# The last 64 rows of a Gram matrix on two 64-column tiles of the array, and its column sum on GpSimd

## Chip, cores, metric

One core of a Trainium2 chip; the three calls of experiments ran on two chips, each beside its own runs of the kernel before. The metric is device microseconds of one execution. All runs quoted here are in the fast state, with a granted TensorE clock of 0.999 or 1.0. Differences of a few tenths of a microsecond in 512 are at stake. The medians alone can't carry them, so the argument rests on stages of the trace: start times of single TensorE matmuls repeat within 0.02 us from run to run in all stages but the first.

## The reference, cut to what matters

```python
xn  = layernorm(x)                          # x: 2048 x 576
q, k, v = split(xn @ wqkv)                  # 32 heads of 18
phi = where(t > 0, t + 1, exp(t)) + 1e-6
kv  = phi(k)^T v     per head
z   = sum over tokens of phi(k)
o   = (phi(q) kv) / (phi(q) z + 1e-6);  attention = o @ wo
out = x + attention + (gelu(xn @ w_gate) * (xn @ w_up)) @ w_down
```

The kernel doesn't compute v. As v = xn Wv, it forms the Gram matrix G = xn^T phi(k) (576 x 576) and then kv = Wv^T G, of which the head blocks are kept.

## The kernel before

Tokens come in 16 tiles of 128. In the **K stage** each tile goes through norm, transpose, the projections k and q (20 matmuls), phi, and part of the Gram matrix. Then follow the rest of the Gram (the **tail**), kv, z, and the FFN in four passes.

A Gram matmul holds 128 columns of xn as weights and streams phi(k) of one tile past them, accumulating in PSUM over the 16 tiles. Row blocks 0 to 3 have 128 rows. Block 4 has 64 rows and one more: a column of ones in xn, whose Gram row is z.

```python
G_A = {   # row block: (bank, column in it, first column of phi(k), width)
    0: [(0, 0, 0, 288), (1, 0, 288, 289)],
    1: [(2, 0, 0, 288), (3, 0, 288, 289)],
    4: [(0, 288, 0, 224), (1, 289, 224, 223), (2, 288, 447, 130)],   # beside 0 and 1, in the banks' remainders
}
G_B = {2: [(4, 0, 0, 288), (5, 0, 288, 289)], 3: [(6, 0, 0, 288), (7, 0, 288, 289)]}

def g_accumulate(n, pieces):
    for kt, ps_ in pieces.items():
        j0, m = (kt * P, P) if kt < 4 else (4 * P, HP + 1)          # 65 weights columns in block 4
        for b, col, d0, w in ps_:
            nc.tensor.matmul(ps_all[:m, b, col:col + w], lhsT=xn[:, n, j0:j0 + m], rhs=pk[:, n, d0:d0 + w], ...)

# K stage: per tile, when its phi(k) is ready:  g_accumulate(n, G_A)    (the last one below)
# tail:
for n in range(NS - 2): g_accumulate(n, {2: G_B[2]})
g_accumulate(NS - 1, G_A)
g_copy(4, ...); g_copy(0, ...); g_copy(1, ...)      # PSUM -> bf16 on DVE and ACT, with 1e-6 of the token sum added
for n in range(NS - 2, NS): g_accumulate(n, {2: G_B[2]})
g_copy(2, ...)
for n in range(NS): g_accumulate(n, {3: G_B[3]})
g_copy(3, ...)
kv_part((0, 1, 4, 2), 0, 1); z_stage(2); kv_part((3,), 0, 1)
# ... FFN
```

`pk` holds phi(k): 16 rows of 578 elements (576 of phi(k), a one, and a pad). In the K stage banks 4 to 7 hold the projections, which is why blocks 2 and 3 wait for the tail. The norm of a later token tile runs on DVE for even tiles and on ACT for odd ones, where GpSimd first computes a small bias. The FFN (`_Unit`) already puts two 64-row tiles side by side.

## Time and profile before

| | before |
|---|---|
| time, median | 514.34 us (first 3 runs 514.33 to 516.33) |
| span of the trace | 512.4 us |
| TensorE busy | 507.3 us, 99% |
| GpSimd (POOL) busy | 6.7 us, 1% |
| K stage, first Gram group to first tail matmul | 46.74 us |
| tail, its first matmul to the first of the FFN | 10.45 us |

The chain that ended last is followed back from the last instruction. Here it is TensorE nearly alone, so a stage's length on TensorE is its price. "Gram group" is one tile's 7 matmuls of `G_A`. The prediction shows the lines.

To read a rate, take distances between starts. A matmul's own duration contains its latency: 286 ns for 288 columns, while the next starts after 121 to 129 ns.

### The profile page before, as it was taken

To read this page: it belongs to the slowest core of one execution; us is meant where nothing else is said; L and a number is where in the kernel's file an instruction comes from. 1 tells how busy PE (TensorE), PEld (TensorE's weight loads), DVE (VectorE), ACT (ScalarE), POOL (GpSimd) and SP (SyncE) were. 2 spreads that over 40 slices of the span, in tenths; PEclk is the share of its full clock that TensorE was granted. 3 is DMA by queue.
4 is the path that set the end of the run, shared out by engine and by line. 5 is a ranking of instruction groups with operands and counts; after the bars stand their busy time and mean duration, and the time that the engine had idled before them with its cause. 6 is when DMAs were issued, how large, how long until landed. Compare 5 with 4: busy or idle time off the path is not lost.

```text
span 512.4 us, 10601 instructions
## 1 busy us (share of the span) xinstructions
PE 507.3 (99%) x4487; PEld 307.7 (60%) x4487; DVE 210.8 (41%) x446; ACT 136.7 (27%) x267; POOL 6.7 (1%) x23
## 2 busy tenths in 40 slices
PE   8999999999999999999999999999999999999997
PEld 7888854444587744444677644444777444445775
DVE  7886446545500045565300254555100356544100
ACT  5887523233310022232100023322000133232000
POOL 3000000000000000000000000000000000000000
PEclk9999999999999999999999999999999999999999
DMA  6643929999700057656300166667100456540000
GB/s 210 145 65 61 249 56 266 289 255 283 175 12 13 1 162 164 157 160 165 103 12 13 56 177 165 164 168 152 43 12 1 142 152 174 163 129 14 13 12 24
DMA packets 118921, 61.18 MB, mean 119 GB/s; under 512 B 25554, under 2 KB 118042, under 8 KB 118874
## 3 DMA queue, kind: packets, MB, share of 16 engines
q1 hardware_dynamic: 118730, 60.36, 45.6%
q8 instruction: 35, 0.57, 0.5%
q10 hardware_dynamic: 144, 0.15, 0.1%
q14 instruction: 12, 0.10, 0.1%
HBM read 52.79 MB, written 2.36 MB: 108 GB/s over the span
## 4 chain that ended last, share of the span: by engine, by line
PE 98%; DMA 1%; DVE 0%; ACT 0%; issue 0%
PE ps_all L309 55%; PE ps_all L639 28%; PE ps_all L254 8%; PE ps_all L285 4%; PE ps_all L644 3%; DMA x_sb<-in_A_x_dram 1%; PE ps_all L627 0%; PE ps_all L356 0%; PE ps_all L590 0%; DVE stats L203 0%; PE ps_all L239 0%; ACT xnT L243 0%; DVE res L653 0%; DVE xn L224 0%; PE ps_all L346 0%
## 5 line engine op out<-in xcount | busy, mean ns | idle before, releaser
L309 PE MATMUL ps_all<-xnT,wg 64*128 64x512 bf16 x1152 | 272.0, 376 | 0.0
L309 PE MATMUL ps_all<-xnT,wu 64*128 64x512 bf16 x1152 | 271.5, 376 | 0.0
L579 ACT ACTIVATE gl<-ps_all 128x512 f32<-128x512 f32 x144 | 86.0, 597 | 311.5 <-PE ps_all L309 311.5
L580 DVE TENSOR_TENSOR hT<-ps_all,gl 128x512 bf16<-128x512 f32 x144 | 99.6, 692 | 131.1 <-ACT gl L579 130.9
L309 PEld LDWEIGHTS <-wu 64*128 64x128 bf16 x1152 | 108.4, 94 | 68.2
L309 PEld LDWEIGHTS <-wg 64*128 64x128 bf16 x1152 | 108.4, 94 | 67.6
L639 PE MATMUL ps_all<-wd_sb,hT 128*128 128x288 bf16 x1152 | 147.1, 286 | 0.0
L639 PEld LDWEIGHTS <-hT 128*128 128x128 bf16 x1152 | 112.3, 98 | 29.3 <-issue 1.2
L653 DVE TENSOR_TENSOR res<-ps_all,x_sb 128x288 bf16<-128x288 f32 x32 | 13.8, 455 | 146.4 <-PE ps_all L644 88.2
L309 PE MATMUL ps_all<-xnT,wr 64*128 64x512 bf16 x288 | 54.7, 377 | 0.0
L254 PE MATMUL ps_all<-wqkv_sb,xnT 128*128 128x288 bf16 x320 | 42.1, 286 | 0.3 <-ACT xnT L243 0.3
L254 PEld LDWEIGHTS <-xnT 128*128 128x128 bf16 x320 | 30.5, 98 | 7.6 <-ACT xnT L243 0.4
L261 ACT ACTIVATE phi_e<-ps_all,neg 128x288 f32<-128x288 f32 x64 | 30.8, 495 | 9.1 <-PE ps_all L254 6.3
L309 PEld LDWEIGHTS <-wr 64*128 64x128 bf16 x288 | 14.1, 94 | 16.8 <-issue 0.2
L285 PE MATMUL ps_all<-hT,xn 128*128 128x288 bf16 (+4 forms) x176 | 22.6, 276 | 0.0
L644 PE MATMUL ps_all<-m_sb,pqT 128*128 128x288 bf16 x128 | 20.9, 286 | 0.0
L285 PEld LDWEIGHTS <-xn 128*128 128x128 bf16 (+1 forms) x176 | 17.6, 101 | 3.9
L266 DVE SCALAR_TENSOR_TENSOR pq<-phi_e,ps_all 128x288 bf16<-128x288 f32 x32 | 14.2, 448 | 7.7 <-ACT phi_e L261 7.4
L266 DVE SCALAR_TENSOR_TENSOR hT<-phi_e,ps_all 128x288 bf16<-128x288 f32 x32 | 14.1, 451 | 2.3 <-ACT phi_e L261 2.3
L644 PEld LDWEIGHTS <-pqT 128*128 128x128 bf16 x128 | 12.5, 98 | 3.2
L203 DVE BATCH_NORM_STATS2 stats<-x_sb 128x6 f32<-128x288 bf16 x32 | 13.6, 440 | 1.8 <-DMA x_sb<-in_A_x_dram 1.8
L389 DVE SCALAR_TENSOR_TENSOR pn<-pq,den_d 128x504 bf16<-128x504 bf16 (+1 forms) x32 | 13.1, 450 | 0.0
(56 smaller groups left out, 104.8 us busy)
## 6 DMA issues: line engine op xcount, KB each, us to landing
wg<-in_B_w_gate_dram SPq DMA_DIRECT2D x72, 256.0 KB, 3.1
wu<-in_B_w_up_dram SPq DMA_DIRECT2D x72, 256.0 KB, 3.6
wd_sb<-in_B_w_down_dram SPq DMA_DIRECT2D x12, 432.0 KB, 4.9
wr<-in_B_w_gate_dram SPq DMA_DIRECT2D x72, 32.0 KB, 2.9
wr<-in_B_w_up_dram SPq DMA_DIRECT2D x72, 32.0 KB, 3.1
out_dram<-res SPq DMA_DIRECT2D x15, 144.0 KB, 1.8
wqkv_sb<-in_A_wqkv_dram SPq DMA_DIRECT2D x3, 576.0 KB, 5.4
x_sb<-in_A_x_dram SPq DMA_DIRECT2D x5, 288.0 KB, 3.2
```

The source lines that it names most:

```text
L203: nc.vector.bn_stats(out=ln_raw[n][:, h, :], in_=x_sb[:, n, h * HALF:(h + 1) * HALF])
L254: nc.tensor.matmul(ps_all[:, KQ_BANK[which] + hf, :HALF], lhsT=xnT[:, kt, n * P:(n + 1) * P], rhs=wqkv_sb[:, kt, c:c + HALF], start=(kt == ...
L261: nc.scalar.activation(out=e[:], in_=ps_all[:, KQ_BANK[which] + hf, :HALF], func=ACT.Exp, bias=neg1[:], scale=1.0,)
L266: nc.vector.scalar_tensor_tensor(out=(pq, pk)[which][:, n, hf * HALF:(hf + 1) * HALF], in0=e_tiles[n, which, hf][:], scalar=1.0, in1=ps_al ...
L285: nc.tensor.matmul(ps_all[:m, b, col:col + w], lhsT=xn[:, n, j0:j0 + m], rhs=pk[:, n, d0:d0 + w], start=(n == 0 and col == 0), stop=(n == ...
L309: return nc.tensor.matmul(self.outs[i], lhsT=self.lhs(i, rows, kt), rhs=self.rhs(i, rows, kt), start=start, stop=stop, skip_group_check=True,)
L389: nc.vector.scalar_tensor_tensor(out=pn_c[:, c0:c1, :nh * DH].rearrange("p c (h e) -> p c h e", e=DH), in0=chunked(heads(pq[:, n, h0 * DH: ...
L579: nc.scalar.activation(out=gl[:], in_=ps_all[:, b[0], :], func=ACT.Gelu_apprx_tanh)
L580: nc.vector.tensor_tensor(out=hT[:, GUB * k + i, :], in0=ps_all[:, b[1], :], in1=gl[:], op=ALU.mult)
L639: nc.tensor.matmul(self.acc(hf), lhsT=hT[:, f, j * P:(j + 1) * P], rhs=wd_sb[:, f, HALVES[hf]], start=(f == 0 and not paired), stop=False, ...
L644: nc.tensor.matmul(self.acc(hf), lhsT=pqT[:, c, self.ts], rhs=m_sb[:, c, HALVES[hf]], start=False, stop=(paired and c == 3), skip_group_ch ...
L653: nc.vector.tensor_tensor(out=self.res[:, hs], in0=self.acc(hf), in1=x_sb[:, self.n, hs], op=ALU.add)
```

## The change

The intent: block 4 uses half of the array's columns but streams all of phi(k). Put its 64 columns of xn into two 64-column tiles of the array. One tile takes the left half of phi(k), the other the right half, side by side. These matmuls are called strips: 16 pairs, one per token tile. Block 4 leaves the K stage; blocks 0, 2 and 1 are accumulated there; the strips come in one stretch in the tail, as a change of tiling has a price. There is no room for the 65th column, so GpSimd sums phi(k) over the tiles and a matmul with ones sums over the partitions. Each half needs its own column of ones for the eps term, hence one at each end of `pk`, and phi(k) moves by one element.

```diff
-    nc.gpsimd.memset(pk[:, :, D:D + 1], 1.0)
+    nc.gpsimd.memset(pk[:, :, 0:1], 1.0)
+    nc.gpsimd.memset(pk[:, :, D + 1:D + 2], 1.0)
...
+    def z_add(n):
+        nc.gpsimd.tensor_tensor(
+            out=z_bf[:] if n == NS - 1 else z_sum[:], in0=pk[:, 0, 1:D + 1] if n == 1 else z_sum[:], in1=pk[:, n, 1:D + 1],
+            op=ALU.add,
+        )
...
-        1: [(2, 0, 0, 288), (3, 0, 288, 289)],
-        4: [(0, 288, 0, 224), (1, 289, 224, 223), (2, 288, 447, 130)],
+        2: [(2, 0, 0, 288), (3, 0, 288, 289)],
+        1: [(0, 288, 0, 224), (1, 289, 224, 223), (2, 288, 447, 130)],
     }
-    G_B = {2: [(4, 0, 0, 288), (5, 0, 288, 289)], 3: [(6, 0, 0, 288), (7, 0, 288, 289)]}
+    G_B = {3: [(4, 0, 0, 288), (5, 0, 288, 289)]}
+    STRIP = ((6, 0, 1, 0), (7, HALF + 1, 0, HALF))
...
+    def g_strip(n):
+        for rows, (b, c0, _, _) in zip((LO, HI), STRIP):
+            nc.tensor.matmul(
+                ps_all[rows, b, 0:HALF + 1], lhsT=xn[:, n, 4 * P:D], rhs=pk[:, n, c0:c0 + HALF + 1],
+                start=(n == 0), stop=(n == NS - 1), skip_group_check=True,
+            )
...
     for n in range(NS - 2):
-        g_accumulate(n, {2: G_B[2]})
+        g_accumulate(n, G_B)
     g_accumulate(NS - 1, G_A)
-    g_copy(4, G_A, (nc.vector, nc.scalar, nc.vector))
     g_copy(0, G_A, (nc.scalar, nc.vector))
-    g_copy(1, G_A, (nc.scalar, nc.vector))
+    g_copy(1, G_A, (nc.vector, nc.scalar, nc.vector))
+    g_copy(2, G_A, (nc.scalar, nc.vector))
+    for n in range(NS):
+        g_strip(n)
+    g_strip_copy()
     for n in range(NS - 2, NS):
-        g_accumulate(n, {2: G_B[2]})
-    g_copy(2, G_B, (nc.scalar, nc.vector))
-    for n in range(NS):
-        g_accumulate(n, {3: G_B[3]})
+        g_accumulate(n, G_B)
     g_copy(3, G_B, (nc.scalar, nc.vector))
-    kv_part((0, 1, 4, 2), 0, 1)
+    kv_part((0, 1, 2, 4), 0, 1)
     z_stage(2)
     kv_part((3,), 0, 1)
```

Cut: the scheduling step of `z_add` (one per tile from tile 1, placed behind the norm or bias of the token tile four ahead), `g_strip_copy`, a second load of the value weights' last 64 rows into the upper partitions, and the z matmul, which now reads `ones` and `z_bf`.

More of the change, by code (lines that the diff above doesn't have):

```diff
@@ L187 @@
     g_sb = apool.tile([P, KT, D], BF16, name="g_sb")
-    nc.gpsimd.memset(g_sb[HP:P, 4, :], 0.0)
-    zsel = const.tile([P, P], BF16, name="zsel")
-    nc.gpsimd.memset(zsel[:], 0.0)
-    nc.gpsimd.memset(zsel[HP:HP + 1, :], 1.0)
+    nc.gpsimd.memset(g_sb[:, 4, :], 0.0)
+    ones = const.tile([P, P], BF16, name="ones")
+    nc.gpsimd.memset(ones[:], 1.0)
+    z_sum = apool.tile([P, D], F32, name="z_sum")
+    z_bf = apool.tile([P, D], BF16, name="z_bf")
+    def z_add(n):
[3 more added lines that the diff above has]
+        )
     mv = persist.tile([P, NS, nc.vector.BN_AGGR_DIM], F32, name="mv")
@@ L266, in kq_phi @@
         nc.vector.scalar_tensor_tensor(
-            out=(pq, pk)[which][:, n, hf * HALF:(hf + 1) * HALF], in0=e_tiles[n, which, hf][:], scalar=1.0,
+            out=(pq, pk)[which][:, n, which + hf * HALF:which + (hf + 1) * HALF], in0=e_tiles[n, which, hf][:], scalar=1.0,
             in1=ps_all[:, KQ_BANK[which] + hf, :HALF], op0=ALU.min, op1=ALU.max,
@@ L282, in g_accumulate @@
         for kt, ps_ in pieces.items():
-            j0, m = (kt * P, P) if kt < 4 else (4 * P, HP + 1)
             for b, col, d0, w in ps_:
                 nc.tensor.matmul(
-                    ps_all[:m, b, col:col + w], lhsT=xn[:, n, j0:j0 + m], rhs=pk[:, n, d0:d0 + w],
+                    ps_all[:, b, col:col + w], lhsT=xn[:, n, kt * P:(kt + 1) * P], rhs=pk[:, n, 1 + d0:1 + d0 + w],
                     start=(n == 0 and col == 0), stop=(n == NS - 1), skip_group_check=True,
                 )
+    def g_strip(n):
[4 more added lines that the diff above has]
+            )
     LO, HI = slice(0, HP), slice(HP, P)
@@ L346, in z_stage @@
             nc.tensor.matmul(
-                ps_all[:, b0 + hf, :HALF], lhsT=zsel[:], rhs=g_sb[:, 4, hf * HALF:(hf + 1) * HALF], start=True, stop=True,
+                ps_all[:, b0 + hf, :HALF], lhsT=ones[:], rhs=z_bf[:, hf * HALF:(hf + 1) * HALF], start=True, stop=True,
             )
-        nc.vector.tensor_copy(out=zb[:].rearrange("p (h d) -> p h d", d=HALF), in_=ps_all[:, b0:b0 + 2, :HALF])
+        nc.vector.tensor_scalar_add(
+            out=zb[:].rearrange("p (h d) -> p h d", d=HALF), in0=ps_all[:, b0:b0 + 2, :HALF], scalar1=S * EPS_ATT,
+        )
     def kv_part(kts, b4, b1):
@@ L457 @@
                      lambda n=n, w=which, h=h: kq_phi(n, w, h))
+        if n > 0:
+            idle = [("norm", n + 4) if n % 2 == 0 else ("bias", n + 4)] if n + 4 < NS else []
+            step(("z", n), "POOL", 1.40, n + 2.0, [("phi", m, 1, h) for m in (0, n) for h in range(2)] + idle,
+                 lambda n=n: z_add(n))
         step(("G", n), "PE", 0.75, n + 1.15, [("phi", n, 1, 0), ("phi", n, 1, 1)], lambda n=n: g_accumulate(n, G_A))
@@ L485, with g_plus_eps, g_strip_copy @@
     nc.scalar.preload_act_table_set("gelu_apprx_tanh_and_others")
+    def g_plus_eps(out_, in_, eps, eng):
+        if eng is nc.scalar:
+            nc.scalar.activation(out=out_, in_=in_, func=ACT.Identity, bias=eps, scale=1.0)
+        else:
+            nc.vector.tensor_scalar_add(out=out_, in0=in_, scalar1=eps)
     def g_copy(kt, pieces, on):
-        m = P if kt < 4 else HP + 1
-        eps = eps_sum[:m, kt:kt + 1]
+        eps = eps_sum[:, kt:kt + 1]
         b, col, _, w = pieces[kt][-1]
-        nc.vector.tensor_scalar_mul(out=eps, in0=ps_all[:m, b, col + w - 1:col + w], scalar1=EPS_ATT)
+        nc.vector.tensor_scalar_mul(out=eps, in0=ps_all[:, b, col + w - 1:col + w], scalar1=EPS_ATT)
         for (b, col, d0, w), eng in zip(pieces[kt][::-1], on):
             w = min(w, D - d0)
-            out_, in_ = g_sb[:m, kt, d0:d0 + w], ps_all[:m, b, col:col + w]
-            if eng is nc.scalar:
-                nc.scalar.activation(out=out_, in_=in_, func=ACT.Identity, bias=eps, scale=1.0)
-            else:
-                nc.vector.tensor_scalar_add(out=out_, in0=in_, scalar1=eps)
+            g_plus_eps(g_sb[:, kt, d0:d0 + w], ps_all[:, b, col:col + w], eps, eng)
+    def g_strip_copy():
+        for rows, (b, _, c0, one) in zip((LO, HI), STRIP):
+            nc.vector.tensor_scalar_mul(out=eps_sum[rows, 4:5], in0=ps_all[rows, b, one:one + 1], scalar1=EPS_ATT)
+        for i, (rows, (b, _, c0, _), eng) in enumerate(zip((LO, HI), STRIP, (nc.scalar, nc.vector))):
+            g_plus_eps(g_sb[rows, 4, i * HALF:(i + 1) * HALF], ps_all[rows, b, c0:c0 + HALF], eps_sum[rows, 4:5], eng)
     load_w(2)
+    nc.sync.dma_start(wqkv_sb[HP:P, 4, 2 * D:], A_wqkv[512:576, 2 * D:])
     for i in range(NWBUF):
```

## The prediction

> **What bounds the kernel now.** I read the page first (busy shares), then the chain that ended last in order of time over the first 75 us, then the groups by form, the stretches and the timeline over the same part, and last the start times of single matmuls. The page says that TensorE is the bound:
>
> ```profile
> span 512.4 us, 10601 instructions
> PE 507.3 (99%) x4487; PEld 307.7 (60%) x4487; DVE 210.8 (41%) x446; ACT 136.7 (27%) x267; POOL 6.7 (1%) x23
> ```
>
> GpSimd (POOL) is nearly free. The chain (start, us, what) shows where the Gram matmuls (L285) stand:
>
> ```profile
> 49.51 0.74 PE ps_all L285 x7
> 50.26 2.45 PE ps_all L254 x20
> 52.71 0.75 PE ps_all L285 x7
> 53.46 2.45 PE ps_all L254 x20
> 55.91 0.75 PE ps_all L285 x7
> 56.66 1.23 PE ps_all L254 x10
> 57.88 8.74 PE ps_all L285 x71
> 66.62 1.11 PE ps_all L356 x20
> 67.73 0.24 PE ps_all L346 x2
> 67.98 0.26 PE ps_all L356 x5
> 68.24 6.79 PE ps_all L309 x61
> ```
>
> In the K stage each token tile is 20 projection matmuls (2.45 us) and 7 Gram matmuls (0.75 us). The tail past it is 71 Gram matmuls, 8.74 us, then the kv products (L356), z (L346) and the FFN (L309). No other engine stands between: the chain is TensorE without a break, so a nanosecond of TensorE taken out of the tail should come off the end. The FFN is also TensorE throughout (chain of the whole: PE 98%), so its start decides its end.
>
> The stretches of one K-stage tile and of the tail (us, then busy time of each engine) show the slack of the others:
>
> ```profile
> 33.53:36.73 3.20, 3.20 (x29) 2.61 (x28) 2.89 (x9) 3.03 (x8) 0.27 (x1) 1.00 0.31 61
> 57.88:66.62 8.74, 8.74 (x75) 6.96 (x73) 3.47 (x11) 3.73 (x6) 0.00 (x0) 1.00 0.49 133
> ```
>
> Columns: PE, PEld, DVE, ACT, POOL. In the K stage DVE and ACT are within 0.2 to 0.3 us of TensorE's 3.20; the tail has them 60% idle. The Gram's forms (busy us, mean ns):
>
> ```profile
> L285 PE MATMUL ps_all<-hT,xn 128*65 128x223 bf16 x16 | 4.2, 260 | 0.0
> L285 PE MATMUL ps_all<-hT,xn 128*65 128x224 bf16 x16 | 4.1, 258 | 0.0
> L285 PE MATMUL ps_all<-hT,xn 128*65 128x130 bf16 x16 | 3.6, 222 | 0.0
> L285 PEld LDWEIGHTS <-xn 128*65 128x65 bf16 x48 | 5.1, 112 | 0.6
> ```
>
> These three matmuls per token tile are what the change replaces: they use 65 of 128 array columns but stream all 577 columns of phi(k). Their mean ns is latency, not rate. By start times, tile 7 spends 123 to 126 ns on each 288 or 289 wide matmul and 95, 99 and 61 ns on these three.
>
> **What the Trainium skill says.** (1) "TensorEngine Tiling (Array Packing)", Key Properties: different tiles load and multiply in parallel; changing the tiling mode drains the array. The trace agrees for row tiles: the FFN's two 64-row matmuls start 3 to 4 ns apart and the next pair 216 ns after the first. A change of mode costs: from L356 to L309 the step is 125 ns where a 72-wide matmul takes 31, and the next pair takes 226; from the pairs of L627 back to full matmuls it is about 95 ns, then 10. No column tile is in this trace. (2) "TensorE: Matmul & The Clock Gate", Part 3 (The mechanism): a weight load overlaps running matmuls only where the row group differs. Both column tiles use all rows, so this speaks against the change. But the trace has full 128-row loads under full 128-row matmuls everywhere (20 projection matmuls in 2.45 us, 122 ns each, with 98 ns loads), so in plain mode they overlap. (3) "GPSIMD Engine Reference", 3.1: an fp32 tensor_tensor of 2048 takes 4497 ns, about 2.6 cycles an element. No GpSimd tensor_tensor is in this trace. My estimate from it for 576: 576 x 2.6 / 1.2 = 1.25 us, with its constant 1.3. (4) "SBUF — State Buffer", Who interferes with whom: a two-input GpSimd operation and a DVE operation in a two-port mode block each other; a DVE operation with one SBUF input outside these modes does not. phi (L266) has one SBUF and one PSUM input and should be safe; the norms on DVE (L224, 420 ns for 576 elements, faster than one per cycle) are candidates. The trace before cannot confirm it.
>
> **The change part by part.**
>
> *Gram, tail rows.* Before, one tile costs four row blocks of two matmuls, about 250 ns each, and the last block at 95 + 99 + 61 = 255: 1255 ns. After, row block 1 takes the three-piece layout (255), blocks 0, 2 and 3 have two pieces (3 x 251), and the strip is one pair of 289 columns side by side, estimated at 126 ns like a single 289: 1134 ns. Saved: 121 ns x 16 = 1.94 us. The count of matmuls stays (11 per tile, 4487 in all).
>
> *K stage.* Still 7 matmuls with the same 1731 columns: 3.20 us per tile. The whole gain must come from the tail.
>
> *Alignment.* phi(k) now starts one element later in its row. The rows are 1156 bytes apart. In the tail before, full matmuls take 122 to 123 ns for n = 0, 4, 8, 12 and 125 to 127 else, and the chain's 7-group is 0.74 us for these n and 0.75 else. So reads at 16-byte boundaries are some 3.5 ns cheaper. After, nearly all reads are off such a boundary: 8 x 16 x 1/4 x 3.5 = +0.11 us in all, of which 0.05 is already in the 251s above; I add 0.07 for the K stage.
>
> *Mode changes.* Into 128x64 tiles and out: 105 + 120 ns as measured on row tiles, +0.22 us, on the path.
>
> *Tail, summed.* From the start of its first matmul (57.72) in the trace to the first FFN matmul (68.17) is 10.45 us. After: block 3 for 14 tiles 14 x 0.251 = 3.51; last K-stage group 0.76; into the mode 0.10; strips 16 x 0.126 = 2.02; out 0.12; block 3 of two tiles 0.50; kv 20 matmuls 1.11; z 0.24; kv 0.36. Sum 8.73, saving 1.72.
>
> *Evictions.* I followed them with the trace's cadence: on DVE a 0.15 us eps and a 0.52 us eviction repeat every 0.62 us, ACT 0.50 us. The last group ends near 62.0, so the evictions of blocks 0, 1, 2 run from 61.7 to 63.8, under the strips, which end at 64.3 with latency. The strip needs two eps (0.18 each) and one eviction on each engine: ready at 65.2. kv of block 4 is fourth in its row and comes up at 65.6. Block 3 (eps 65.1, evictions to 65.8) is needed at 66.1. Both have some 0.3 us to spare: no stall. The last copy of xnT into the upper rows landed at 64.0, and 0.55 us more of DMA issue for the second load of the value weights brings that to 64.6, before the FFN at 66.45.
>
> *z on GpSimd.* 15 adds of 1.3 us, about 20 us over a 50 us stage; the last after phi(15), near 57 to 59, well before z is wanted at 65.8. Around tile 8 the bias is done at 34.2, two adds fit to 36.9, and the norm on DVE starts at 37.1: just clear. DVE's phi has about 1.5 us until its bank is wanted, so a brush would be absorbed.
>
> Net: -1.72 + 0.07 = -1.65. 514.34 - 1.65 = 512.7 us.
>
> **The rivals.** (a) *Column tiles do not overlap*, or their loads stand in between. Then a strip costs two matmuls (250 ns or more): the strips take 4.0 us instead of 2.0, the gain is gone and the mode changes stay: 514.7. For it: the skill's sentence in (2). Against it: its sentence in (1), the row tiles' exact overlap, and plain-mode overlap. A partial form (exposed loads of some 27 ns each; 126-, 72- and 65-wide loads take 137, 114 and 112 ns, 0.4 ns a column) would give 513.5. I give both together 15%. (b) *GpSimd slows the K stage*: adds longer than estimated collide with norms, or hold back a bias and so ACT, whose slack is 0.2 us per tile. A tenth of a microsecond per tile gives 514.2 or more. For it: the near touch at 36.9. Against: 1.5 us of buffer slack in phi. 12%. (c) *A new wait in the tail*: the strip or block 3 evicted late, TensorE waits 0.2 to 0.5 us: 513.0. The margins of 0.3 us are thin: 25%. (d) A DMA hides it anyway: the weights for the first FFN block landed by 57; 5%.
>
> **Range and chances.** The gain is 0.3% in the main case and the worst rivals cost 0.3 to 0.5%, so a 2% verdict is almost surely "same". Rival (c) pulls to 513.0, (a) and (b) to 514.2 and more. One of the three runs before was 2 us high, so I leave a little room: 512.1 to 514.3.
>
> **What would show it.** Right: strip matmuls as 128*64 with 289 columns, two starts 3 to 4 ns apart and 122 to 130 ns to the next pair; the K stage still 3.20 us per tile; FFN start near 66.4 instead of 68.2; L285 still x176; POOL about 26 us busy with x38; no wait of TensorE for DVE or ACT before kv. Wrong: strip starts 120 ns apart; a tile of the K stage over 3.25 us; idle time of PE before L356; GpSimd adds over 2 us.

## The result, and the profile after

The changed kernel takes **512.54 us** (median of 6, 512.38 to 512.91), the kernel before 514.34 (6 runs in all). The ratio is 0.9959, 95% interval 0.9944 to 0.9974: "same" by the 2% measure, and 1.8 us faster by the medians. A ratio is the mean time of one kernel's fast runs over that of the other's of the same rounds, so it isn't quite the ratio of the medians.

The page of the changed kernel, first two lines:

```profile
span 510.9 us, 10642 instructions
PE 505.0 (99%) x4487; PEld 305.4 (60%) x4487; DVE 211.2 (41%) x447; ACT 136.8 (27%) x267; POOL 24.7 (5%) x38
```

TensorE has as many matmuls as before and is busy 2.3 us less; POOL has 15 instructions and 18 us more.

The changed kernel's chain in order of time (start, us, what) around the tail. L293 is the Gram, L262 the projections, L300 the strips, L373 kv, L361 z, L324 the FFN:

```profile
56.09 0.75 PE ps_all L293 x7
56.84 1.23 PE ps_all L262 x10
58.07 4.27 PE ps_all L293 x35
62.34 2.11 PE ps_all L300 x32
64.44 0.61 PE ps_all L293 x4
65.05 1.11 PE ps_all L373 x20
66.17 0.24 PE ps_all L361 x2
66.41 0.26 PE ps_all L373 x5
66.67 8.52 PE ps_all L324 x77
```

Where 71 Gram matmuls took 8.74 us there are now 35 + 32 + 4, in 4.27 + 2.11 + 0.61 = 6.99. The 32 strip matmuls take 2.11 us, 66 ns each, though a 289-wide matmul alone needs some 123 to 127. kv, z and kv again are as long as before, and no other engine stands in the chain.

Forms of the changed kernel in the first 75 us (busy us, mean ns, idle before):

```profile
L300 PE MATMUL ps_all<-hT,xn 128*64 128x289 bf16 x32 | 2.2, 288 | 0.0
L300 PEld LDWEIGHTS <-xn 128*64 128x64 bf16 x32 | 1.8, 110 | 0.2
L197 POOL TENSOR_TENSOR z_sum<-z_sum,hT 128x576 f32<-128x576 f32 x13 | 16.2, 1244 | 4.7 <-DVE hT L274 4.4
```

One after the other at 123 ns, 32 such matmuls would keep TensorE busy for 3.9 us; these do so for 2.2 us, so they lie side by side. (The 288 ns of one is again latency.) By single start times the two of a pair begin 3 to 4 ns apart at first and up to 16 ns at the end, and after the first (148 ns) the pairs follow at 122 to 125 ns.

The two stages as stretches, the kernel before first (us, then busy us and count of PE, PEld, DVE, ACT, POOL; clock, DMA share, GB/s):

```profile
11.15:57.88 46.73, 46.73 (x397) 38.17 (x396) 36.77 (x101) 37.04 (x90) 1.81 (x7) 1.00 0.55 118
57.88:68.24 10.36, 10.36 (x101) 8.49 (x100) 4.38 (x14) 4.23 (x7) 0.00 (x0) 1.00 0.42 112
```

and the changed kernel:

```profile
11.27:58.07 46.80, 46.80 (x397) 37.99 (x396) 36.84 (x101) 37.12 (x90) 19.60 (x22) 1.00 0.53 115
58.07:66.67 8.60, 8.60 (x100) 7.13 (x100) 4.63 (x15) 4.23 (x7) 0.47 (x1) 1.00 0.58 157
```

The K stage is 0.07 us longer, the tail 1.76 us shorter (10.36 - 8.60), TensorE is busy in all of both, and GpSimd now works in the K stage.

Start times of single matmuls give the same division more sharply, for all kernels of this study. The columns are: first projection to first Gram; K stage; tail; from the first FFN matmul to the end; and the profiled run's time less its span as the trace has it (the page rounds the span to 0.1 us).

| kernel | first | K stage | tail | FFN to end | outside span |
|---|---|---|---|---|---|
| before | 4.17 | 46.735 | 10.453 | 444.267 | 1.97 |
| b1 before again | 4.75 | 46.735 | 10.454 | 444.262 | 1.98 |
| changed | 4.36 | 46.801 | 8.700 | 444.335 | 1.77 |
| e0 changed again | 4.70 | 46.803 | 8.700 | 444.335 | 1.77 |
| e1 one tile, then the other | 3.97 | 46.804 | 10.206 | 444.336 | 1.77 |
| e2 strips spread | 3.97 | 46.802 | 14.339 | 444.331 | 1.76 |
| e3 z on DVE | 3.98 | 47.767 | 8.700 | 444.335 | 1.95 |
| e4 one z addition | 4.50 | 46.807 | 8.700 | 444.340 | 1.79 |
| e5 phi(k) aligned | 4.12 | 46.665 | 8.615 | 444.320 | 1.80 |
| e6 before, aligned | 4.03 | 46.669 | 10.325 | 444.253 | 1.96 |
| e7 z additions twice | 4.58 | 46.898 | 8.700 | 444.329 | 1.76 |
| e8 strips by fours | 3.97 | 46.803 | 8.727 | 444.333 | 1.76 |
| e9 aligned again | 4.55 | 46.667 | 8.614 | 444.335 | 1.77 |

The first column varies by 0.8 us whatever the kernel (there the first projections wait for the loads of x and the weights), and with it the times of single runs. The next three repeat within 0.02 us for the same kernel. From the first FFN matmul on, all starts of before and changed agree within 3 ns, to the last one 440.79 us later, so the 0.07 us of the fourth column lies behind the last matmul. The trace shows where. Counted from the first FFN matmul, the last output transfer is issued at 441.60 us and lands at 443.18 to 443.19 us in both. SyncE ends with six waits for semaphores. In the kernel before, the second of them holds until this landing and four follow; in the changed kernel it is the first and five follow. A wait is some 62 ns, and every later record stands 63 to 68 ns later. So the 0.07 us hangs on which closing wait the last transfer was given, and is no work of the changed stages.

### The profile page after: what moved, and what is told of

It is laid out like the page before. It is cut to its first block, busy times and chain, and to the rows that moved or that the text cites. A ratio compares the mean times of both kernels' runs of the same rounds, so it can differ in the third digit from the quotient of the medians.

```text
span 510.9 us, 10642 instructions
## 1 busy us (share of the span) xinstructions
PE 505.0 (99%) x4487; PEld 305.4 (60%) x4487; DVE 211.2 (41%) x447; ACT 136.8 (27%) x267; POOL 24.7 (5%) x38
## 4 chain that ended last, share of the span: by engine, by line
PE 98%; DMA 1%; SPq 0%; DVE 0%; issue 0%
PE ps_all L324 55%; PE ps_all L668 28%; PE ps_all L262 7%; PE ps_all L293 3%; PE ps_all L673 3%; DMA wqkv_sb<-in_A_wqkv_dram 1%; PE ps_all L656 0%; PE ps_all L300 0%; PE ps_all L373 0%; PE ps_all L619 0%; SPq L93 0%; SPq L108 0%; DVE res L682 0%; SPq L107 0%; PE ps_all L361 0%
## 5 line engine op out<-in xcount | busy, mean ns | idle before, releaser
L324 PE MATMUL ps_all<-xnT,wg 64*128 64x512 bf16 x1152 | 271.9, 376 | 0.0
L324 PE MATMUL ps_all<-xnT,wu 64*128 64x512 bf16 x1152 | 271.5, 376 | 0.0
L324 PEld LDWEIGHTS <-wu 64*128 64x128 bf16 x1152 | 108.3, 94 | 68.3
L324 PEld LDWEIGHTS <-wg 64*128 64x128 bf16 x1152 | 108.3, 94 | 67.7
L324 PE MATMUL ps_all<-xnT,wr 64*128 64x512 bf16 x288 | 54.6, 376 | 0.0
L262 PE MATMUL ps_all<-wqkv_sb,xnT 128*128 128x288 bf16 x320 | 42.1, 286 | 0.5 <-ACT xnT L251 0.3
L262 PEld LDWEIGHTS <-xnT 128*128 128x128 bf16 x320 | 30.5, 98 | 7.9 <-ACT xnT L251 0.4
L324 PEld LDWEIGHTS <-wr 64*128 64x128 bf16 x288 | 14.0, 94 | 16.8 <-issue 0.2
L293 PE MATMUL ps_all<-hT,xn 128*128 128x288 bf16 (+4 forms) x144 | 18.8, 274 | 0.0
L197 POOL TENSOR_TENSOR z_sum<-z_sum,hT 128x576 f32<-128x576 f32 x13 | 16.2, 1244 | 4.7 <-DVE hT L274 4.4
L293 PEld LDWEIGHTS <-xn 128*128 128x128 bf16 x144 | 14.0, 98 | 3.6 <-issue 0.2
```

Source lines behind the costliest of these rows:

```text
L197: nc.gpsimd.tensor_tensor(out=z_bf[:] if n == NS - 1 else z_sum[:], in0=pk[:, 0, 1:D + 1] if n == 1 else z_sum[:], in1=pk[:, n, 1:D + 1], ...
L262: nc.tensor.matmul(ps_all[:, KQ_BANK[which] + hf, :HALF], lhsT=xnT[:, kt, n * P:(n + 1) * P], rhs=wqkv_sb[:, kt, c:c + HALF], start=(kt == ...
L293: nc.tensor.matmul(ps_all[:, b, col:col + w], lhsT=xn[:, n, kt * P:(kt + 1) * P], rhs=pk[:, n, 1 + d0:1 + d0 + w], start=(n == 0 and col = ...
L324: return nc.tensor.matmul(self.outs[i], lhsT=self.lhs(i, rows, kt), rhs=self.rhs(i, rows, kt), start=start, stop=stop, skip_group_check=True,)
```

## The experiments

My theory: the gain is the overlap of the two column tiles in the tail, less two changes of tiling; GpSimd's work is hidden; nothing new waits. Rivals: the tiles don't overlap and something else gained; GpSimd costs the K stage something; the evictions or the mode changes eat part. e1, e2, e4 and e5 came in one call and share its runs of before (median 514.51); e0, e3, e7 and e8 came in a second (514.47), b1, e6 and e9 in a third (514.40).

**e1: the same strips, all of one tile first.**

```diff
-    for n in range(NS):
-        g_strip(n)
+    for which in range(2):
+        for n in range(NS):
+            g_strip(n, which)
```

Cut: `g_strip` gets the argument `which` (0 is the lower tile, 1 the upper) and issues that tile's matmul alone; e8 uses the same.

> Same 32 strip matmuls in the same 128x64 mode, but all 16 of the lower column tile first, then all 16 of the upper one, so that no two neighbours can run side by side. My theory (the gain is the overlap of the two column tiles): strips of one tile start 122 to 126 ns apart, the strip stretch grows from 2.1 to about 4.0 us, the kernel from 512.5 to 514.4 to 514.5 us, the time of the kernel before. Rival (the gain comes from streaming 289 instead of 577 columns per instruction order or from the shorter list of pieces, not from overlap): under 0.5 us slower than the changed kernel.

Measured: 514.23 us (21 runs), ratio to before 0.9995 (0.9989 to 1.0002). The gain is gone. Its chain:

```profile
57.85 4.27 PE ps_all L293 x35
62.12 3.61 PE ps_all L300 x32
65.74 0.61 PE ps_all L293 x4
```

The strips take 3.61 us instead of 2.11, and nothing else moved. So the gain is the overlap: instruction count, piece layout and GpSimd are as in the changed kernel and give nothing without it. The tail grew by 1.51 us, not by the 1.9 expected. By start times, the first 12 strips come singly, then four pairs come some 5 to 31 ns apart, and the last 12 singly: the last four of the lower tile ran beside the first four of the upper one. So there are 12 more steps than in the changed kernel, not 16, and 12 x 0.124 = 1.49.

**e8: strips in groups of four per tile.** It tests what e1's four pairs suggest.

```diff
-    for n in range(NS):
-        g_strip(n)
+    for n0 in range(0, NS, 4):
+        for which in range(2):
+            for n in range(n0, n0 + 4):
+                g_strip(n, which)
```

> Strips in groups: four matmuls of the lower column tile, then four of the upper, and so on. In e1 the last four of the lower tile ran beside the first four of the upper, which cost 1.5 us instead of 1.9. My theory now (the array starts a matmul of an idle tile while some three earlier ones of the busy tile still wait): groups of four overlap almost fully, the tail stays within 0.2 us of 8.70. Rival (overlap needs neighbours; e1's four were an effect of its end): only one pair at each of the 7 changes of tile overlaps, 24 to 25 steps of 123 ns instead of 16, +1.0 to +1.1 us, as far as 9.8 us.

Measured: 512.40 us, ratio 0.9965 (0.9953 to 0.9977). The chain has

```profile
62.03 2.13 PE ps_all L300 x32
```

and the tail is 8.727 us, 0.03 more than in pairs. The pairs now start 13 to 39 ns apart. Overlap doesn't need neighbours in the program: a matmul of the other tile starts while three earlier ones of this tile are still waiting. With starts in strict program order, groups of four could overlap only at their edges, which was the rival's 9.8 us. That the scheduler of the build had put the pairs together is a rival too; it is ruled out, as the programs of e1 and e8, built again from their kernels, keep the order of the source. In e1 sixteen of one tile stood in a row, and only the last four ran beside the other tile: no more than three were ever overtaken.

**e2: strips spread over the tail.**

```diff
     for n in range(NS - 2):
         g_accumulate(n, G_B)
+        g_strip(n)
...
-    for n in range(NS):
+    for n in range(NS - 2, NS):
         g_strip(n)
```

> The strip of each of the first 14 token tiles runs right after block 3 of this tile instead of in one stretch, so the array changes mode 15 times in and out instead of once. My theory (a change of mode costs some 0.11 us each way on the path, measured 0.091 + 0.022 in and about 0.112 out in the changed kernel): 14 more pairs of changes at about 0.23 us = +3.2 us, 515.7 us. Rival (the drain is hidden by the weights loaded ahead, or was a one-time cost): within 0.5 us of the changed kernel, 513.0 or less.

Measured: 518.13 us, ratio 1.0068; the tail is 14.34 us, 5.64 longer instead of the expected 3.2. A part of its chain and TensorE's own waits in it:

```profile
65.83 0.35 PE ps_all L293 x2
66.18 0.25 PE ps_all L300 x2
66.43 0.35 PE ps_all L293 x2
66.78 0.25 PE ps_all L300 x2
```

```profile
PE ps_all L373 <- DVE g_sb L513: 0.8, 2, 0.6
PE ps_all L300 <- DVE pq L274: 0.5, 2, 0.3
PE ps_all L373 <- ACT g_sb L511: 0.3, 1, 0.3
```

One round (two full matmuls and a pair of strips) takes 0.600 us from start to start where 0.375 would do without a change of tiling, so in and out costs 0.225 us. 14 of them are 3.15 us, as expected. The other 2.5 us are waits that I hadn't thought of. Placed this early, the first strips wait for phi(q) of the last tile to leave banks 6 and 7 (0.87 us of start times). At the end the evictions of blocks 0 to 2 no longer run beneath a long stretch of strips. They and the evictions behind them come too late for kv, which waits before its first matmul (0.74 us), around the strips' rows (0.44 us) and before block 3 (0.36 us), about 1.6 us together with smaller delays. So the single stretch does two things: it pays the change of tiling once, and it covers the evictions.

**e4: one addition of z instead of 15.** The result is wrong on purpose (relative error 0.08).

```diff
     def z_add(n):
+        if n < NS - 1:
+            return
         nc.gpsimd.tensor_tensor(
-            out=..., in0=pk[:, 0, 1:D + 1] if n == 1 else z_sum[:], in1=pk[:, n, 1:D + 1],
+            out=..., in0=pk[:, 0, 1:D + 1], in1=pk[:, n, 1:D + 1],
```

In the diffs `...` stands for code that is cut.

> Wrong result on purpose: only the last of the 15 GpSimd additions of z is left (tile 0 plus tile 15). My theory (the additions are hidden, GpSimd costs the K stage nothing): same time as the changed kernel within 0.15 us, K-stage tile still 3.20 us. Rival (the additions hold DVE's norms or a bias back a little and the 0.07 us that the K stage grew is theirs, or more): 0.1 to 0.5 us faster than the changed kernel, K stage back to 46.73 us from first to last Gram group.

Measured: 512.85 us (512.37 to 513.23), ratio 0.9965 as for e0. The median misses the expected 0.15 us, but medians carry the varying first stage (4.50 us in this profile), so the stages decide. The K stage is 46.807 us, to be set beside 46.801 and 46.803 with all additions. GpSimd's additions cost the K stage nothing, and its 0.07 us over the kernel before isn't theirs; e5 will show whose it is.

**e7: each addition twice**, the first into a spare tile.

```diff
     def z_add(n):
+        nc.gpsimd.tensor_tensor(
+            out=z_idle[:], in0=pk[:, 0, 1:D + 1] if n == 1 else z_sum[:], in1=pk[:, n, 1:D + 1], op=ALU.add,
+        )
         nc.gpsimd.tensor_tensor(
```

> Each addition of z is done twice on GpSimd (the first into a spare tile), result unchanged: GpSimd needs some 5 us of every 6.4, and its operations now must lie across the norms on DVE and the biases. My theory (the additions are harmless because they fit between bias and norm with 0.2 to 0.4 us to spare, and phi has about 1.5 us of buffer): the K stage grows by less than 0.5 us. Rival (any touch of GpSimd with the norms stalls DVE and so TensorE): the K stage grows by 1 to 3 us. The waits of DVE's norms and of ACT's norms for the bias should show the touch in either case.

Measured: 512.54 us, ratio 0.9965; the K stage is 46.90 us, 0.10 more. The norms on DVE between 11 and 58 us (busy us, mean ns), first before, then changed, then e7:

```profile
L224 DVE TENSOR_SCALAR xn<-x_sb,mv,rstd 128x576 bf16<-128x576 bf16 x6 | 2.5, 419 | 0.0
```

```profile
L232 DVE TENSOR_SCALAR xn<-x_sb,mv,rstd 128x576 bf16<-128x576 bf16 x6 | 2.6, 442 | 0.0
```

```profile
L237 DVE TENSOR_SCALAR xn<-x_sb,mv,rstd 128x576 bf16<-128x576 bf16 x6 | 3.7, 613 | 0.0
```

So the touch is there. In e7 one norm took 1373 ns and another 650 instead of about 430. These timelines of e7 show the first, DVE and then POOL:

```profile
20.24 1.37 DVE L237 TENSOR_SCALAR xn<-x_sb,mv,rstd 128x576 bf16<-128x576 bf16 x1
```

```profile
20.25 1.20 POOL L199 TENSOR_TENSOR z_idle<-z_sum,hT 128x576 f32<-128x576 f32 x1
```

The norm ends 0.16 us after the addition that began beside it. The Trainium skill's "SBUF — State Buffer", Who interferes with whom, is borne out: a GpSimd addition blocks a norm on DVE. (Which of these two was first can't be told from starts 0.01 us apart.) phi on DVE isn't touched: for phi(k) it takes 453 ns in the changed kernel and in e7. In the changed kernel one norm is stretched as well, from 429 to 572 ns, at 25.7 us; in e4, without the addition, it takes 429. Even a norm held for 0.9 us moved the K stage by only 0.1. Slack between DVE and TensorE takes the rest; that it is the buffers of phi, as predicted, no run tests alone. The rival of 1 to 3 us falls.

**e3: the additions on DVE.**

```diff
-        nc.gpsimd.tensor_tensor(
+        nc.vector.tensor_tensor(
             out=z_bf[:] if n == NS - 1 else z_sum[:], ...
```

> The 15 additions of z on DVE instead of GpSimd, in the same places of the program. My theory (they are free only because GpSimd is idle; DVE is busy 2.7 to 2.9 of 3.20 us per tile up to about tile 9): an addition on DVE of some 0.7 us makes DVE need 3.4 to 3.6 us per tile for the first 10 tiles or so, the K stage grows by 2 to 4 us, the kernel to 514.5 to 516.5 us. Rival (DVE has slack that the busy figures hide, or the later tiles, where DVE is busy 1.8 of 3.20, take it up): within 0.5 us of the changed kernel.

Measured: 513.74 us (21 runs), ratio 0.9986 (0.9979 to 0.9992); the K stage is 47.77 us, 0.97 longer. A stretch of it (columns as above):

```profile
33.62:36.83 3.21, 3.05 (x26) 2.33 (x25) 3.21 (x10) 3.04 (x8) 0.27 (x1) 1.00 0.26 51
```

DVE is busy without a break and TensorE isn't. The direction is as expected, the size isn't: half of the lower end of 2 to 4 us. By start times of the Gram groups, five tiles grew by more than 0.05 us (to 3.26 to 3.53 us), while the others stayed at 3.20 to 3.22. An addition took 0.74 to 0.77 us on DVE, as estimated; but my estimate charged every early tile with its full excess, and only five paid. That work in hand carried TensorE over the others is likely and wasn't tested. The choice of GpSimd is worth 0.97 us here, over half of what the strips gain.

**e5, e9: phi(k) on a 16-byte boundary.** The last open item of the K stage is its 0.07 us.

```diff
-PKW = 578
+PKW = 592
+PO = 8                      # phi(k) starts at element 8; ones at 7 and at 584
...
-                    ps_all[:, b, col:col + w], lhsT=..., rhs=pk[:, n, 1 + d0:1 + d0 + w],
+                    ps_all[:, b, col:col + w], lhsT=..., rhs=pk[:, n, PO + d0:PO + d0 + w],
```

Cut: the ones, phi, the additions of z and the strips move with `PO` in the same way.

> phi(k) starts at element 8 of a row of 592 elements (1184 bytes), so all 288 and 289 wide full Gram matmuls read from a 16-byte boundary. My theory (a moving read off such a boundary costs some 3.5 ns a matmul): six full matmuls per token tile x 16 x 3.5 ns = -0.34 us against the changed kernel, 512.2 us, and start distances of 122 to 123 ns where they were 126. Rival (the 3.5 ns belong to something else, such as the eviction bank or the odd weight block): distances stay at 126 and the time stays at 512.5.

> e5 once more, as the candidate for a version that beats both: K stage 46.67 us and tail 8.62 us as in its first profile; 1.9 to 2.2 us faster than the kernel before of the same call.

Measured: 512.45 us (ratio 0.9958) and 512.54 us (0.9959). The stages: K 46.665 and 46.667 (0.14 less than changed), tail 8.615 and 8.614 (0.09 less). The chain of e5 has these, to be set beside 0.75 and 4.27 in the changed kernel:

```profile
52.48 0.74 PE ps_all L294 x7
57.64 4.18 PE ps_all L294 x35
```

In the tail the starts of full Gram matmuls are now 122 to 124 ns apart where 126 was the rule. So alignment is real, and worth 0.22 us rather than 0.34. In the K stage each pair of 288 and 289 wide matmuls got faster by 4 ns, not 7 (122.8 + 127.3 before this edit, 122.5 + 123.4 after). The medians can't tell e5 and e9 from the changed kernel (512.44 and 512.54), and e9's 1.86 us against before just misses the expected 1.9; the stages can. It is the best version of the study, by 0.22 us of stages.

**e6: the kernel before with aligned rows.**

```diff
-PKW = 578
+PKW = 584
```

> The kernel before with rows of phi(k) 584 instead of 578 elements apart (1168 bytes, a multiple of 16), nothing else. If reads off a 16-byte boundary cost what e5 suggests: the K stage shrinks by about 0.1 us, the tail by 62 matmuls x 3/4 x 3.5 ns = 0.16 us, together some 0.25 us faster than before. Rival (alignment is of no account): all stages as before within 0.03 us.

Measured: 514.24 us, ratio 0.9995 (0.9987 to 1.0003). K stage 46.669 (-0.07), tail 10.325 (-0.13), 0.19 us in all, where 0.25 was expected. The same effect stands in the old kernel, so it belongs to the reads and not to the strips.

**e0 and b1: both kernels again.**

> The changed kernel, unaltered, as the control beside the other three of this call: 1.6 to 1.9 us faster than the kernel before; from first tail matmul to first FFN matmul 8.70 us, K stage 46.80 us from its first to its last Gram group; only the first 11 us (loads) may vary from run to run.

> The kernel before, unaltered, for a second profile of it. The stages of the profiles (K stage -0.07, tail +1.75 us saved, FFN -0.07 us) add up to 1.62 us, the medians differ by 1.8 to 2.0 us. The rest should lie in the first 11 us (from the first projection matmul to the first Gram group, 3.97 to 4.70 us in the changed kernel's runs) or outside the span (time less span 1.97 us in the one profile of before, 1.76 to 1.80 us in the changed ones). If it is by kernel, this profile has again 1.9 us or more outside its span; if it varies by run, it has about 1.8 us or another start.

e0: 512.44 us, ratio 0.9965 (0.9953 to 0.9978), stages as in the first profile; by the medians 2.03 us faster than before, a little over the expected 1.9. b1: 514.66 us, ratio 1.0004, stages as in the first profile, and again 1.98 us outside its span. So the 0.2 us outside the span go by kernel and not by run. The changed kernel and all its variants that add on GpSimd have 1.76 to 1.80. Both profiles of before, e6 and e3 (z on DVE) have 1.95 to 1.98. All runs of the experiments say the same: their means are 1.76 to 1.78 and 1.95 to 1.97. Why is open, as no record lies outside the span. It can be the addition itself or something that goes with it, such as GpSimd working later in the program; e4 shows that one late addition is enough.

## Why the prediction was right, step by step

512.7 us was predicted, 512.54 measured. By its steps:

- **Strips and Gram in the tail.** Tail predicted 8.73 us, measured 8.70 in the changed kernel and in e0. e1 shows that the overlap is the cause: with four pairs left of sixteen it takes 10.21.
- **Mode changes.** Predicted 0.105 in and 0.12 out from row tiles; e2 measures 0.225 for both on column tiles. The lines that the prediction names give only 95 + 10 = 105 ns for the way out, so its 120 has no source there. Row tiles thus cost 0.21 us and column tiles 0.225: the price carries over from one kind of tile to the other, and the exact hit is luck.
- **K stage.** Predicted +0.07 us from alignment; measured +0.066 to 0.068. e4 rules GpSimd out, and e5 takes the 0.07 and another 0.07 away by alignment alone. Alignment is the cause, but the size was hit in part by luck. By the prediction only the four token tiles that had read from a 16-byte boundary (0, 4, 8, 12) lose; their Gram groups lost 25 ns together, and the eleven others, off the boundary before and after, 33 ns that it didn't have. The 3.5 ns for every matmul was too even, too: in the K stage the cost showed behind one of each two full matmuls, and the strip pairs followed at 122 to 125 ns though at least one of each two reads off the boundary.
- **Evictions.** No wait of TensorE was predicted, and there was none, but the margins were mis-sized. kv of block 4 had about 0.28 us to spare, as estimated. Block 3's eviction ended at 66.18 us, only 0.07 before its first kv matmul started at 66.25, where 0.3 was estimated. The DVE chain of two eps and one eviction was a little slower than the cadence I carried over.
- **z on GpSimd.** 1.3 us per addition estimated; 1.14 to 1.30 measured, the median of the 13 in the middle 1.205. So the estimate held. POOL busy 24.7 us with 38 instructions (about 26 and 38 predicted). The last addition ended at 58.5. "Just clear" of the norms was wrong for one tile (429 to 572 ns); "a brush would be absorbed" was right, as e7 shows with a much harder one.
- **The sum.** -1.75 in the tail and +0.07 in the K stage, together -1.69 us, with -1.65 predicted. Two terms no step of the prediction had: +0.07 us behind the last matmul and -0.2 us outside the span. With them the stages give -1.8, and the medians -1.80 (-2.03 in e0's rounds, where the first stage varies).
- **The rivals.** (a) no overlap, or loads in between: ruled out by the pairs at 122 to 125 ns and by e1. (b) GpSimd slows the K stage: ruled out by e4. (c) a new wait in the tail: none, but the 0.07 us of block 3 shows how near it was, and e2 what such waits cost. (d) a DMA hides it: the FFN began when kv ended.

## What to carry to other kernels

A matmul with 64 weight columns (fewer weren't tried) can have half of its streaming time back if its moving operand is split over two column tiles, provided the tiled matmuls stand together: here a change of tiling in and out costs as much as nearly two 288-wide matmuls. Put such a stretch where evictions must run anyway: spread out, the strips of e2 lost 1.6 us to evictions that the stretch had covered, beside the 3.15 us of the changes. And look for the idle engine first when something small must move (GpSimd took z at no cost to the K stage, DVE would have taken back 0.97 us), and check that the moving rows still start on the 16-byte boundary they did.

## What the Trainium skill lacked or had wrong

- "TensorEngine Tiling (Array Packing)", Key Properties, says that a change of mode drains the array, but gives no cost for it. Here 0.225 us for in and out (e2), about half each way.
- "TensorE: Matmul & The Clock Gate", Part 3, The mechanism, says in its list that weight loads overlap running matmuls only where the row group differs. Taken alone this is too narrow: the column tiles share all rows, each pair needs two loads of 110 ns, and the pairs follow at 122 to 125 ns, so the loads are hidden. The paragraph above that list does allow it for weights that go to the background buffer; the prediction left that out when it held the sentence against the change.
- The same section has the matmuls in strict program order at start and end. e8's 32 strips in groups of four took 2.13 us where that order allows overlap only at the edges of the groups; so across column tiles matmuls start out of program order. e8 shows it past three waiting matmuls, and e1, with sixteen in a row, past no more than three.
- No page has the cost of a matmul's moving operand that starts off a 16-byte boundary ("SBUF — State Buffer" notes 16-byte lines, for strides): up to 4 ns on a 288-wide matmul here, 0.22 us in this kernel (e5) and 0.19 in the one before (e6). "SBUF — State Buffer", Operand start alignment, says that it is about legality and timed nothing.
- No page explains the 0.2 us outside the span that go with an elementwise GpSimd operation in the program (1.76 to 1.80 against 1.95 to 1.98); it stays open.
